# Zero-padded K and V, four one-bank score buffers and a fused feed-forward stage in a retention + SoLU kernel

## The chip, the cores and the metric

The kernel runs on one core of one Trainium2 chip. Times are device microseconds (us) of that core. PE is TensorE's matmuls, PEld its weight loads, DVE is VectorE, ACT is ScalarE, POOL is GpSimd. A run counts as faster or slower when it differs by more than 2% from the kernel before.

## The reference, cut to what matters

Retention (attention with a decay mask and no softmax) over 8 batches, 8 heads, 576 positions and a head size of 64, then a feed-forward part over the 4608 tokens: 512 → 1024, SoLU, LayerNorm, 1024 → 512.

```python
scores = (q @ k.T) / sqrt(64)                      # per batch and head, 576 x 576
ret    = scores * where(i >= j, gamma[h] ** (i - j), 0)
attn   = ret @ v                                   # 576 x 64
x      = attn of all heads side by side            # 4608 x 512
h      = x @ w_in                                  # 4608 x 1024
solu   = h * softmax(h)
ln     = (solu - mean) / sqrt(var + 1e-6) * g_ln
out    = ln @ w_out                                # 4608 x 512
```

## The kernel before

For each pair of heads the kernel transposes Q and K with PE into tiles whose partitions 0 to 63 hold one head and 64 to 127 the other. For each head it makes five key blocks of scores (the mask is causal, so block `kb` needs only `576 - 128*kb` columns), multiplies each by the decay table on DVE, and then makes the products with V ("PV" below) that add up in `opv`. The rows cut out are marked.

```python
tc.tile_pool(name="a_st", bufs=6) as a_st,
tc.tile_pool(name="ps_tr", bufs=2, space=bass.MemoryType.PSUM) as ps_tr,
tc.tile_pool(name="ps_sc", bufs=2, space=bass.MemoryType.PSUM) as ps_sc,   # two tiles of two banks
tc.tile_pool(name="ps_pv", bufs=1, space=bass.MemoryType.PSUM) as ps_pv,
# ... loads and casts of a batch, transposes and copies of a pair of heads cut ...
for hh in range(2):
    h = h0 + hh
    dr = slice(hh * D, (hh + 1) * D)              # 64 of the 128 partitions
    st_tiles = []
    for kb in range(SB):                          # SB = 5
        sps = ps_sc.tile([128, S], FP32, tag="sps")
        for c0 in range(0, ncols, 512):           # kb 0 needs 512 + 64 columns
            nc.tensor.matmul(out=sps[0:kb_rows, c0:c1],
                lhsT=kT[dr, 128 * kb:128 * kb + kb_rows],          # 64 rows x 128 columns
                rhs=qT[dr, 128 * kb + c0:128 * kb + c1], start=True, stop=True)
        st = a_st.tile([128, S], FP16, tag="st")
        nc.vector.tensor_tensor(out=st[0:kb_rows, 0:ncols], in0=sps[0:kb_rows, 0:ncols],
            in1=Mt[0:kb_rows, h, 0:ncols], op=ALU.mult)
        st_tiles.append(st)
    for kb in range(SB - 1):
        nc.tensor.matmul(out=opv[dr, 128 * kb:512],
            lhsT=v16[0:128, kb, h],                                # 128 rows x 64 columns
            rhs=st_tiles[kb][0:128, 0:512 - 128 * kb],
            start=(kb == 0), stop=(kb == SB - 2))
    # ... five matmuls of 64 columns into opv[dr, 512:S] cut ...
# ... after all batches: four groups of nine blocks of 128 tokens ...
#     stage 1 of each block: hps = x w_in (PE), exp (ACT), t = hps * e, statistics (DVE), transposes (PE)
#     then for the group: Ln and Exp (ACT), and for each block ops = lnT w_out (PE), osb (ACT), store
```

The softmax here doesn't subtract the row's maximum and nothing guards it: scores larger than these inputs give would overflow.

Of the kernel before, what the change touches and what calls it, by code (L numbers as in the profile page):

```python
# [17 lines left out]
def kernel(  # L18
# [10 lines left out]
    nc = tc.nc  # L29
# [47 lines left out]
    xT = const.tile([128, NDMB, NT], FP16)  # L77

    npart = 128
    with (  # L80
        tc.tile_pool(name="a_in", bufs=2) as a_in,
        tc.tile_pool(name="a_tr", bufs=4) as a_tr,
        tc.tile_pool(name="a_st", bufs=6) as a_st,
        tc.tile_pool(name="ps_tr", bufs=2, space=bass.MemoryType.PSUM) as ps_tr,
        tc.tile_pool(name="ps_sc", bufs=2, space=bass.MemoryType.PSUM) as ps_sc,
        tc.tile_pool(name="ps_pv", bufs=1, space=bass.MemoryType.PSUM) as ps_pv,
    ):
        for b in range(B):
            qn = a_in.tile([128, SB, H, D], FP32, tag="qn")
            kn = a_in.tile([128, SB, H, D], FP32, tag="kn")  # L90
            vn = a_in.tile([128, SB, H, D], FP32, tag="vn")
            q16 = a_in.tile([128, SB, H, D], FP16, tag="q16")
            k16 = a_in.tile([128, SB, H, D], FP16, tag="k16")
            v16 = a_in.tile([128, SB, H, D], FP16, tag="v16")
# [16 lines left out]
            nc.vector.tensor_copy(out=v16[:, 0:SB - 1], in_=vn[:, 0:SB - 1])  # L111
            nc.vector.tensor_copy(out=v16[0:SBL, SB - 1], in_=vn[0:SBL, SB - 1])

            for hp in range(HP):
                h0 = 2 * hp
                pass
                qT_ps = ps_tr.tile([128, S], FP16, tag="trps")
                kT_ps = ps_tr.tile([128, S], FP16, tag="trps")
# [9 lines left out]
                kT = a_tr.tile([128, S], FP16, tag="kT")  # L128
                nc.scalar.activation(out=qT, in_=qT_ps, func=ACT.Copy)
                nc.scalar.activation(out=kT, in_=kT_ps, func=ACT.Copy)  # L130

                opv = ps_pv.tile([128, S], FP32, tag="opv")
                for hh in range(2):
                    h = h0 + hh
                    dr = slice(hh * D, (hh + 1) * D)
                    pass
                    st_tiles = []
                    for kb in range(SB):
                        kb_rows = 128 if kb < SB - 1 else SBL
                        ncols = S - 128 * kb  # L140
                        sps = ps_sc.tile([128, S], FP32, tag="sps")
                        for c0 in range(0, ncols, 512):
                            c1 = min(ncols, c0 + 512)
                            nc.tensor.matmul(  # L144
                                out=sps[0:kb_rows, c0:c1],
                                lhsT=kT[dr, 128 * kb:128 * kb + kb_rows],
                                rhs=qT[dr, 128 * kb + c0:128 * kb + c1],
                                start=True, stop=True)
                        st = a_st.tile([128, S], FP16, tag="st")
                        nc.vector.tensor_tensor(  # L150
                            out=st[0:kb_rows, 0:ncols],
                            in0=sps[0:kb_rows, 0:ncols],
                            in1=Mt[0:kb_rows, h, 0:ncols],
                            op=ALU.mult)
                        st_tiles.append(st)
                    for kb in range(SB - 1):
                        nc.tensor.matmul(  # L157
                            out=opv[dr, 128 * kb:512],
                            lhsT=v16[0:128, kb, h],
                            rhs=st_tiles[kb][0:128, 0:512 - 128 * kb],  # L160
                            start=(kb == 0), stop=(kb == SB - 2))
                    for kb in range(SB):
                        kb_rows = 128 if kb < SB - 1 else SBL
                        nc.tensor.matmul(  # L164
                            out=opv[dr, 512:S],
                            lhsT=v16[0:kb_rows, kb, h],
                            rhs=st_tiles[kb][0:kb_rows, 512 - 128 * kb:S - 128 * kb],
                            start=(kb == 0), stop=(kb == SB - 1))
# [3 lines left out]
    GRP = 9  # L172
    ngrp = (NTB + GRP - 1) // GRP
    with (
        tc.tile_pool(name="m_sb", bufs=3) as m_sb,
        tc.tile_pool(name="m_ln", bufs=GRP + 2) as m_ln,
        tc.tile_pool(name="m_sc", bufs=4) as m_sc,
        tc.tile_pool(name="m_gs", bufs=2) as m_gs,
        tc.tile_pool(name="ps_h", bufs=4, space=bass.MemoryType.PSUM) as ps_h,
        tc.tile_pool(name="ps_ln", bufs=2, space=bass.MemoryType.PSUM) as ps_ln,  # L180
        tc.tile_pool(name="ps_o", bufs=2, space=bass.MemoryType.PSUM) as ps_o,
    ):
        for gi in range(ngrp):
            blocks = list(range(gi * GRP, min(NTB, (gi + 1) * GRP)))
            sqG = m_gs.tile([128, GRP], FP32, tag="sq")
            rstdG = m_gs.tile([128, GRP], FP32, tag="rstd")
            lnT_list = []
            for li, t in enumerate(blocks):
                tcols = slice(t * 128, (t + 1) * 128)
                e16 = m_sb.tile([128, DFF], FP16, tag="e16")  # L190
                t32 = m_sb.tile([128, DFF], FP32, tag="t32")
                zp = m_sc.tile([128, 2], FP32, tag="zp")
                stats = m_sc.tile([128, 2, 6], FP32, tag="stats")
                for c in range(2):
                    fcs = slice(c * 512, (c + 1) * 512)
                    hps = ps_h.tile([128, 512], FP32, tag="hps")
                    for i in range(NDMB):
                        nc.tensor.matmul(  # L198
                            out=hps, lhsT=xT[:, i, tcols],
                            rhs=w_in16[:, i, fcs],  # L200
                            start=(i == 0), stop=(i == NDMB - 1))
                    nc.scalar.activation(  # L202
                        out=e16[:, fcs], in_=hps, func=ACT.Exp,
                        accum_out=zp[:, c:c + 1])
                    nc.vector.tensor_tensor(  # L205
                        out=t32[:, fcs], in0=hps, in1=e16[:, fcs], op=ALU.mult)
                    nc.vector.bn_stats(out=stats[:, c], in_=t32[:, fcs])  # L207
                mv = m_sc.tile([128, 2], FP32, tag="mv")
                nc.vector.bn_aggr(out=mv, in_=stats)
                zs = m_sc.tile([128, 2], FP32, tag="zs")  # L210
                nc.vector.tensor_scalar(
                    out=zs[:, 0:1], in0=zp[:, 0:1], scalar1=zp[:, 1:2],
                    scalar2=1e-9, op0=ALU.add, op1=ALU.add)
                nc.scalar.activation(out=zs[:, 1:2], in_=zs[:, 0:1],
                                     func=ACT.Square)
                nc.vector.tensor_scalar(
                    out=sqG[:, li:li + 1], in0=zs[:, 1:2], scalar1=1e-6,
                    scalar2=mv[:, 1:2], op0=ALU.mult, op1=ALU.add)
                negmu = m_sc.tile([128, 1], FP32, tag="negmu")
                nc.vector.tensor_scalar(  # L220
                    out=negmu, in0=mv[:, 0:1], scalar1=-1.0, scalar2=None,
                    op0=ALU.mult)
                ln16 = m_sb.tile([128, DFF], FP16, tag="ln16")
                for c in range(2):
                    fcs = slice(c * 512, (c + 1) * 512)
                    nc.vector.tensor_scalar(  # L226
                        out=ln16[:, fcs], in0=t32[:, fcs], scalar1=negmu,
                        scalar2=None, op0=ALU.add)
                lnT_ps = ps_ln.tile([128, NFFB, 128], FP16, tag="lnT")
                for f in range(NFFB):  # L230
                    nc.tensor.transpose(  # L231
                        out=lnT_ps[:, f], in_=ln16[:, f * 128:(f + 1) * 128],
                        identity=ident)
                lnT = m_ln.tile([128, NFFB, 128], FP16, tag="lnTs")
                nc.scalar.activation(out=lnT, in_=lnT_ps, func=ACT.Copy)  # L235
                lnT_list.append(lnT)
            nblk = len(blocks)
            lnv = m_gs.tile([128, GRP], FP32, tag="lnv")
            nc.scalar.activation(out=lnv[:, 0:nblk], in_=sqG[:, 0:nblk],
                                 func=ACT.Ln)  # L240
            nc.scalar.activation(out=rstdG[:, 0:nblk], in_=lnv[:, 0:nblk],
                                 func=ACT.Exp, scale=-0.5)
            for li, t in enumerate(blocks):
                tcols = slice(t * 128, (t + 1) * 128)
                lnT = lnT_list[li]
                ops = ps_o.tile([128, DM], FP32, tag="ops")
                for f in range(NFFB):
                    nc.tensor.matmul(  # L248
# [36 lines left out]
```

## Time and profile before

| | us |
|---|---|
| timed, median of 3 runs | 542.65 (540.79 to 542.81) |
| profiled span | 536.3 |
| loading, to the first decay product | 43 |
| attention (43 to 349) | 306 |
| feed-forward (349 to 536) | 187 |

The page of the kernel before: the span, the busy time of each engine, the clock granted to TensorE in 40 slices (tenths of full speed), and the costliest groups. A group's columns are line, engine, operation, output and input, shapes, count; then busy us and mean ns of one; then the idle time before them and what ended it.

```profile
span 536.3 us, 6044 instructions
PE 437.5 (82%) x2144; PEld 195.2 (36%) x2144; DVE 295.3 (55%) x704; ACT 226.9 (42%) x401; POOL 0.2 (0%) x4
PEclk9999999999999999999999999999989999999959
L150 DVE TENSOR_TENSOR st<-sps,Mt 128x576 f16<-128x576 f32 (+4 forms) x320 | 149.7, 487 | 160.5 <-PE sps L144 151.5
L144 PE MATMUL sps<-qT,kT 64*128 64x512 f16 (+5 forms) x384 | 136.8, 406 | 20.3 <-DVE st L150 20.3
L157 PE MATMUL opv<-st,v 128*64 128x512 f16 (+3 forms) x256 | 106.2, 474 | 5.5 <-DVE v L111 5.5
```

The windows view of the kernel before, attention in the first line and feed-forward in the second. Its columns are the stretch and its length; busy us and count of PE, PEld, DVE, ACT and POOL; the granted clock; the busy share of the DMA engines; GB/s.

```profile
43.00:349.00 306.00, 280.26 (x1266) 120.58 (x1265) 161.41 (x336) 91.92 (x121) 0.00 (x0) 1.00 0.45 82
349.00:536.30 187.30, 154.53 (x865) 73.03 (x864) 129.95 (x360) 122.84 (x269) 0.00 (x0) 0.95 0.14 51
```

The timeline of the kernel before, PE alone. Its columns are start us, length us, engine, line, operation, output and input, tile (rows x columns of the array), input shape and count.

```profile
49.19 1.27 PE L157 MATMUL opv<-st,v 128*64 128x512 f16 x4 [0.47 <-DVE v L111]
...
329.60 0.63 PE L157 MATMUL opv<-st,v 128*64 128x512 f16 x1
330.17 0.34 PE L144 MATMUL sps<-qT,kT 64*128 64x192 f16 x1
330.44 0.53 PE L157 MATMUL opv<-st,v 128*64 128x384 f16 x1
330.89 0.26 PE L144 MATMUL sps<-qT,kT 64*64 64x64 f16 x1
...
376.41 1.89 PE L198 MATMUL hps<-w_in,xT 128*128 128x512 f16 x8 [0.29 <-DVE t L205]
```

PE is 280.26 of 306 us "busy" in attention, yet the starts are far apart: a PV of 512 columns starts at 329.60 and the score matmul after it at 330.17, 0.57 us later. In the feed-forward part eight matmuls of 512 columns take 1.89 us, the last of them 0.38, so they start (1.89 − 0.38)/7 = 0.216 us apart. The page and the windows show the clock in attention as full (9, 1.00). The first line of the timeline shows four PV matmuls (512, 384, 256 and 128 columns) taking 1.27 us.

### The profile page before, as it was taken

The page shows a single profiled execution, that of the slowest core. Times are in us where ns is not written, and L with a number is a line of the kernel's source. Part 1 is how long each engine was busy: PE and PEld are TensorE (multiplying, and loading weights), DVE is VectorE, ACT ScalarE, POOL GpSimd, SP SyncE. Part 2 cuts the span into 40 slices and gives each one's busy share as a digit, 9 for nine tenths or more (in the row PEclk, how much of TensorE's full clock was granted, in tenths as well). Part 3 has the DMA queues.
Part 4 walks back from the last instruction along what each step waited for, and adds up shares of the span by engine and source line. Part 5 has one row for each costly group of instructions (what it writes and reads, how often), then busy time and mean ns, then how long its engine had stood idle before and what let it go on. Part 6 is the DMA issues. An engine that isn't in the chain of part 4 may idle for free.

```text
span 536.3 us, 6044 instructions
## 1 busy us (share of the span) xinstructions
PE 437.5 (82%) x2144; PEld 195.2 (36%) x2144; DVE 295.3 (55%) x704; ACT 226.9 (42%) x401; POOL 0.2 (0%) x4
## 2 busy tenths in 40 slices
PE   0009998998998998998989988898699789879756
PEld 0004333343443343343344343344244334434322
DVE  0204555536545546545555545579937984984920
ACT  2134333243143152341332330066847777676653
POOL 0000000000000000000000000000000000000000
PEclk9999999999999999999999999999989999999959
DMA  9599999454444444444000000000030021022013
GB/s 301 190 204 215 209 216 198 86 111 88 88 90 88 89 88 89 88 89 89 0 2 0 1 1 0 1 0 2 8 144 26 2 109 68 1 90 90 0 55 122
DMA packets 121678, 44.74 MB, mean 83 GB/s; under 512 B 114480, under 2 KB 114480, under 8 KB 121648
## 3 DMA queue, kind: packets, MB, share of 16 engines
q1 hardware_dynamic: 121648, 44.35, 37.6%
q8 instruction: 17, 0.28, 0.2%
q14 instruction: 13, 0.11, 0.1%
HBM read 34.90 MB, written 9.44 MB: 83 GB/s over the span
## 4 chain that ended last, share of the span: by engine, by line
PE 63%; DVE 17%; ACT 6%; DMA 5%; issue 5%; SPq 4%; DVEq 0%; ACTq 0%
PE opv L157 17%; PE sps L144 17%; PE ops L248 11%; DVE st L150 5%; PE opv L164 5%; PE hps L198 4%; PE qT_ps L121 4%; PE kT_ps L124 4%; DMA wt<-in_moe_w_out_dram 3%; DVE stats L207 3%; SPq L98 3%; DVE t L205 3%; DVE ln L226 3%; ACT lnT L235 2%; DVE v L111 2%
## 5 line engine op out<-in xcount | busy, mean ns | idle before, releaser
L150 DVE TENSOR_TENSOR st<-sps,Mt 128x576 f16<-128x576 f32 (+4 forms) x320 | 149.7, 487 | 160.5 <-PE sps L144 151.5
L144 PE MATMUL sps<-qT,kT 64*128 64x512 f16 (+5 forms) x384 | 136.8, 406 | 20.3 <-DVE st L150 20.3
L157 PE MATMUL opv<-st,v 128*64 128x512 f16 (+3 forms) x256 | 106.2, 474 | 5.5 <-DVE v L111 5.5
L169 ACT ACTIVATE xT<-opv 128x576 f16<-128x576 f32 x32 | 20.8, 650 | 160.3 <-PE opv L164 160.3
L248 PE MATMUL ops<-w_out,lnT 128*128 128x512 f16 x288 | 71.3, 395 | 11.0 <-ACT osb L252 9.9
L198 PE MATMUL hps<-w_in,xT 128*128 128x512 f16 x288 | 71.7, 382 | 9.5 <-DVE t L205 6.1
L205 DVE TENSOR_TENSOR t<-hps,e 128x512 f32<-128x512 f32 x72 | 47.2, 660 | 27.0 <-ACT e L202 27.0
L157 PEld LDWEIGHTS <-v 128*64 128x64 f16 x256 | 29.0, 135 | 79.0 <-issue 58.1
L121 PE MATMUL qT_ps<-ident,q 128*128 128x128 f16 (+1 forms) x160 | 27.3, 292 | 35.7 <-ACT q L103 35.7
L144 PEld LDWEIGHTS <-kT 64*128 64x128 f16 (+1 forms) x384 | 35.6, 115 | 56.1 <-issue 49.6
L202 ACT ACTIVATE e<-hps 128x512 f16<-128x512 f32 x72 | 42.9, 600 | 22.8 <-PE hps L198 21.2
L207 DVE BATCH_NORM_STATS2 stats<-t 128x6 f32<-128x512 f32 x72 | 48.3, 685 | 0.0
L248 PEld LDWEIGHTS <-lnT 128*128 128x128 f16 x288 | 28.8, 101 | 42.9 <-issue 13.1
L198 PEld LDWEIGHTS <-xT 128*128 128x128 f16 x288 | 27.6, 98 | 41.2 <-issue 15.1
L164 PE MATMUL opv<-st,v 128*64 128x64 f16 (+1 forms) x320 | 41.2, 249 | 0.0
L164 PEld LDWEIGHTS <-v 128*64 128x64 f16 (+1 forms) x320 | 32.7, 158 | 17.7 <-issue 13.5
L235 ACT ACTIVATE lnT<-lnT_ps 128x1024 f16<-128x1024 f16 x36 | 36.2, 1022 | 5.3 <-PE lnT_ps L231 4.7
L130 ACT ACTIVATE kT<-kT_ps 128x576 f16<-128x576 f16 x32 | 20.8, 650 | 36.7 <-PE kT_ps L124 36.7
L252 ACT ACTIVATE osb<-ops,rstdG 128x512 f32<-128x512 f32 x36 | 24.5, 688 | 27.1 <-PE ops L248 24.1
L231 PE MATMUL lnT_ps<-ident,ln 128*128 128x128 f16 x288 | 26.5, 225 | 7.4 <-DVE ln L226 6.7
L121 PEld LDWEIGHTS <-q 128*128 128x128 f16 (+1 forms) x160 | 14.4, 123 | 49.8 <-ACT q L103 35.7
L226 DVE TENSOR_SCALAR ln<-t,negmu 128x512 f16<-128x512 f32 x72 | 31.3, 477 | 0.2
(28 smaller groups left out, 204.6 us busy)
## 6 DMA issues: line engine op xcount, KB each, us to landing
out_dram<-osb SPq DMA_DIRECT2D x36, 256.0 KB, 2.0
qn<-in_q_dram SPq DMA_DIRECT2D x32, 256.0 KB, 4.9
kn<-in_k_dram SPq DMA_DIRECT2D x32, 256.0 KB, 5.0
vn<-in_v_dram SPq DMA_DIRECT2D x32, 256.0 KB, 4.8
Mt<-decay_tab SPq DMA_DIRECT2D x1, 2304.0 KB, 8.7
wt<-in_moe_w_in_dram SPq DMA_DIRECT2D x4, 512.0 KB, 6.6
wt<-in_moe_w_out_dram SPq DMA_DIRECT2D x8, 256.0 KB, 3.7
qn<-in_q_dram SPq DMA_DIRECT2D x8, 128.0 KB, 4.7
```

The source lines that it names most:

```text
L121: nc.tensor.transpose(out=qT_ps[:, 128 * c:128 * c + rows], in_=q16[0:rows, c, h0:h0 + 2], identity=ident[0:rows, 0:rows])
L144: nc.tensor.matmul(out=sps[0:kb_rows, c0:c1], lhsT=kT[dr, 128 * kb:128 * kb + kb_rows], rhs=qT[dr, 128 * kb + c0:128 * kb + c1], start=Tru ...
L150: nc.vector.tensor_tensor(out=st[0:kb_rows, 0:ncols], in0=sps[0:kb_rows, 0:ncols], in1=Mt[0:kb_rows, h, 0:ncols], op=ALU.mult)
L157: nc.tensor.matmul(out=opv[dr, 128 * kb:512], lhsT=v16[0:128, kb, h], rhs=st_tiles[kb][0:128, 0:512 - 128 * kb], start=(kb == 0), stop=(kb ...
L164: nc.tensor.matmul(out=opv[dr, 512:S], lhsT=v16[0:kb_rows, kb, h], rhs=st_tiles[kb][0:kb_rows, 512 - 128 * kb:S - 128 * kb], start=(kb == ...
L198: nc.tensor.matmul(out=hps, lhsT=xT[:, i, tcols], rhs=w_in16[:, i, fcs], start=(i == 0), stop=(i == NDMB - 1))
L202: nc.scalar.activation(out=e16[:, fcs], in_=hps, func=ACT.Exp, accum_out=zp[:, c:c + 1])
L205: nc.vector.tensor_tensor(out=t32[:, fcs], in0=hps, in1=e16[:, fcs], op=ALU.mult)
L207: nc.vector.bn_stats(out=stats[:, c], in_=t32[:, fcs])
L226: nc.vector.tensor_scalar(out=ln16[:, fcs], in0=t32[:, fcs], scalar1=negmu, scalar2=None, op0=ALU.add)
L235: nc.scalar.activation(out=lnT, in_=lnT_ps, func=ACT.Copy)
L248: nc.tensor.matmul(out=ops, lhsT=lnT[:, f], rhs=w_out16[:, f], start=(f == 0), stop=(f == NFFB - 1))
```

## The change

The intent is that every matmul use the full 128x128 array (the last key block of a head has only 64 keys and keeps narrow tiles), that PE run ahead of DVE, and that feed-forward work sit between batches. Four parts:

1. **Padding.** K of each head is copied into a tile of 128 rows whose other 64 rows are zero; V gets 128 columns of which 64 are zero. Scores then use all of Q's 128 rows (the other head's rows meet zeros), and both heads of a pair add up into one `opv` of 128 partitions.
2. **Score buffers.** Two score tiles of two banks become four of one bank; the 576-column block is cut into 512 + 64 with a decay product each. `hps` and `ops` share these four.
3. **Fusion.** One scope of pools; a feed-forward group of nine blocks follows every second batch.
4. Smaller: fp32 inputs in one buffer instead of two, `m_sb` 3 → 2, a pool of four for `osb`.

```diff
+    v16z = [const.tile([128, SB, HP, 2, 2 * D], FP16, name=f"v16z{n}") for n in range(2)]   # memset to 0
+    kz = [[const.tile([128, S], FP16, name=f"kz{hh}{n}") for n in range(NZ)] for hh in range(2)]  # memset to 0
-        tc.tile_pool(name="ps_sc", bufs=2, space=bass.MemoryType.PSUM) as ps_sc,
+        tc.tile_pool(name="ps_big", bufs=4, space=bass.MemoryType.PSUM) as ps_big,
+        def moe_group(blocks):  # ... the feed-forward part, moved here; hps and ops from ps_big, cut ...
...
-                nc.scalar.activation(out=kT, in_=kT_ps, func=ACT.Copy)
+                for hh in range(2):
+                    r = slice(hh * D, (hh + 1) * D)
+                    nc.scalar.activation(out=kzs[hh][r], in_=kT_ps[r, 0:S], func=ACT.Copy)
...
-                        sps = ps_sc.tile([128, S], FP32, tag="sps")
                         for c0 in range(0, ncols, 512):
+                            sps = ps_big.tile([128, 512], FP32, tag="big")
-                                lhsT=kT[dr, 128 * kb:128 * kb + kb_rows],
-                                rhs=qT[dr, 128 * kb + c0:128 * kb + c1],
+                                lhsT=kzs[hh][:, 128 * kb:128 * kb + kb_rows],
+                                rhs=qT[:, 128 * kb + c0:128 * kb + c1],
-                        nc.vector.tensor_tensor(out=st[0:kb_rows, 0:ncols], ...)     # once for each kb
+                            nc.vector.tensor_tensor(out=st[0:kb_rows, c0:c1], ...)   # once for each c0
...
-                            out=opv[dr, 128 * kb:512],
-                            lhsT=v16[0:128, kb, h],
-                            start=(kb == 0), stop=(kb == SB - 2))
+                            out=opv[:, 128 * kb:512],
+                            lhsT=v16[0:128, kb, hp, hh],
+                            start=(kb == 0 and hh == 0), stop=(kb == SB - 2 and hh == 1))
...
+            if b % 2 == 1:
+                blk0 = (b - 1) * S // 128
+                moe_group(list(range(blk0, blk0 + GRP)))
```

## The prediction

> **What bounds the kernel now.** The span is 536 us (timed 542.65). By the timeline: 43 us of loading, 306 us of attention (43 to 349; 38.6 us a batch: 8 heads of about 4.25 us plus 4 for casts and transposes), 187 us of feed-forward (groups of nine blocks, 42 to 53 us each). In attention PE shows as 93% busy, but is not streaming. A head's eight large matmuls have 2,752 columns; at the feed-forward part's 0.216 us per 512 columns that is 1.16 us, plus seven small ones and five transposes at 0.1: 2.3 us, against 4.25. The timeline shows why: wherever a score matmul (64x128 tile) meets a PV matmul (128x64 tile), the next start is late. PV 512 to score: 0.56 us; PV 384: 0.46; score 192 to PV: 0.27, though 192 columns need 0.08. Five PV matmuls of one shape start 0.1 us apart. The Trainium skill ("TensorEngine Tiling (Array Packing)", Key Properties) says that changing the tiling mode drains TensorE; this trace agrees, at 0.2 to 0.35 us a change. By the waits view DVE is idle 151 us for scores, PE 20 us for the only two score buffers.
>
> **What the change does.** (1) K and V are zero-padded, so every matmul is a 128x128 tile: same columns, no mode changes. (2) Four one-bank score tiles instead of two; the 576-column product becomes 512 + 64, about 0.15 us more DVE per head. (3) Two half-height K copies for one: +0.65 us ACT per pair, not critical. (4) A feed-forward group follows every second batch. By the instruction order, DVE and PE still do attention, then group, then attention; this hides little and loses something: today group n+1's first blocks run during group n's output matmuls. (5) Single-buffered f32 inputs: casts stay a batch ahead, no cost.
>
> **Estimate.** From the trace: score to DVE start 0.29 us after streaming, DVE end to PE 0.05, DVE 0.69/0.22/0.62/0.49/0.36/0.22 (2.3 back to back). Order: score 512, 64, 448, PV 512, score 320, PV 384, score 192, PV 256, score 64, PV 128, five small PVs. Following it: DVE starts at 0.50, PV 512 at 1.24, PV 384 at 1.97, PV 256 at 2.41, PV 128 at 2.91, next head at 3.47. So 3.5 us a head, bound by the PE-DVE-PE loop, transposes fitting in its waits. A batch: 28 + 2 for casts = 30; attention 240 (-66).
>
> Feed-forward: DVE-bound at 3.63 us a block, 33 us; table loads 3, about 39 remaining output matmuls 8.5, next transposes, copies and first score 3.5, entry 2: 50 each, 202 in all (+15).
>
> Sum: 43 + 240 + 202 = 485 span, plus 5 as today: **488 us**, range **455 to 517**. Chances: faster by over 2% 0.95, within 2% 0.04, slower 0.01.
>
> **What would show it.** Right: score-to-PV spacing falls to columns/2.4 GHz where nothing is waited for; a head takes 3.3 to 3.7 us; DVE idle on scores falls to about 70 us; PE's waits on the decay product become the limit; DVE has gaps of 12 to 16 us at each group-to-attention switch; DVE busy about 310 us. Wrong: spacing unchanged (drains not the cause); head time near 2.6 (loop hidden, total near 440); group over 55 us.
>
> **What would make it wrong.** Transposes landing on the loop (+0.5 us a head, +30 us); strided V casts slower; lower granted clock after the waits; ACT blocked behind casts waiting for DMA; better overlap at group borders than read from the order.

## The result, and the profile after

| | before | after |
|---|---|---|
| timed, median | 542.63 us (537.3 to 544.17, 15 runs) | 409.25 us (405.62 to 411.94, 12 runs) |
| profiled span | 536.3 | 403.6 |
| attention | 306 | 167.2, in four stages |
| feed-forward | 187.3 | 193.4, in four stages |

The ratio is 0.7562 (0.7532 to 0.7592). Every ratio here is the mean time of one kernel's fast runs over that of the other's of the same rounds, so it isn't quite the ratio of the medians quoted. The prediction said 488 us, with a range from 455; the change gained much more than that.

The page of the kernel after, the same lines as above.

```profile
span 403.6 us, 6141 instructions
PE 311.4 (77%) x2144; PEld 164.4 (41%) x2144; DVE 284.5 (70%) x784; ACT 243.6 (60%) x433; POOL 13.0 (3%) x14
L241 DVE TENSOR_TENSOR st<-sps,Mt 128x512 f16<-128x512 f32 (+5 forms) x384 | 138.6, 425 | 74.7 <-PE sps L236 70.0
L236 PE MATMUL sps<-qT,kz 128*128 128x512 f16 (+5 forms) x384 | 89.6, 287 | 4.4 <-DVE st L241 2.8
L248 PE MATMUL opv<-st,v16z 128*128 128x512 f16 (+3 forms) x256 | 69.6, 300 | 6.3 <-ACT xT L260 4.9
```

The same counts of score and PV matmuls take a third less busy time each (136.8 → 89.6 and 106.2 → 69.6). DVE's idle time for scores fell from 151.5 to 70.0 us, PE's waits for a decay product from 20.3 to 2.8. The 70.0 us are mostly not in attention's loop: 16.8 are the wait for the very first scores (16.7 in before) and 39.5 the three changes from a group back to attention. What is left, 13.8 us, was 134.8 in before.

The windows view of the kernel after: attention of two batches and a feed-forward group in turn (the first two of the four rounds).

```profile
43.00:88.20 45.20, 40.34 (x302) 23.21 (x303) 37.59 (x104) 27.70 (x37) 0.00 (x0) 1.00 1.12 190
88.20:136.80 48.60, 39.44 (x238) 18.96 (x237) 34.02 (x94) 36.50 (x75) 0.00 (x0) 1.00 0.58 130
136.80:178.20 41.40, 38.57 (x313) 22.21 (x310) 37.64 (x104) 27.73 (x39) 0.00 (x0) 1.00 0.81 141
178.20:226.70 48.50, 39.83 (x229) 18.76 (x227) 33.94 (x96) 31.63 (x70) 0.00 (x0) 0.96 0.45 103
```

All four attention stages take 45.2 + 41.4 + 40.2 + 40.4 = 167.2 us, the four groups 48.6 + 48.5 + 46.7 + 49.6 = 193.4. In attention PE and DVE are now both close to full: 38.57 and 37.64 of 41.40 us.

The timeline of the kernel after: PE over one head.

```profile
62.31 0.38 PE L248 MATMUL opv<-st,v16z 128*128 128x512 f16 x1 [0.22 <-ACT xT L260]
62.62 0.22 PE L236 MATMUL sps<-qT,kz 128*64 128x64 f16 x1
62.77 0.34 PE L248 MATMUL opv<-st,v16z 128*128 128x384 f16 x1
62.94 0.38 PE L236 MATMUL sps<-qT,kz 128*128 128x512 f16 x1
63.16 0.27 PE L248 MATMUL opv<-st,v16z 128*128 128x256 f16 x1
63.27 0.19 PE L236 MATMUL sps<-qT,kz 128*128 128x64 f16 x1
63.29 0.22 PE L248 MATMUL opv<-st,v16z 128*128 128x128 f16 x1
63.35 0.41 PE L255 MATMUL opv<-st,v16z 128*128 128x64 f16 x5
63.70 0.36 PE L236 MATMUL sps<-qT,kz 128*128 128x448 f16 x1
```

The score matmuls of 512 and 64 columns at 62.94 and 63.27 are the *next* head's: they stand between this head's PV matmuls. Its 448-column scores follow at 63.70, before any of its own PVs. So DVE has the next head's scores in hand before this head is done. (The tile of 128x64 at 62.62 is the block of 64 keys: the padding doesn't widen it.) The timeline of the kernel after, DVE alone, shows it:

```profile
136.84 2.13 DVE L241 TENSOR_TENSOR st<-sps,Mt 128x512 f16<-128x512 f32 x6 [12.76 <-PE sps L236]
...
159.26 17.34 DVE L241 TENSOR_TENSOR st<-sps,Mt 128x512 f16<-128x512 f32 x48
```

Forty-eight decay products, eight heads of six, run in 17.34 us without an idle stretch: 2.17 us a head. The prediction had 3.5. (The first line shows the gap of 12.76 us at a change from a group back to attention, which the prediction did expect.)

### The clock records

The trace also holds the throttle's own records. Each says from when, for how long, and at which share of full speed. The first ones of four kernels, in us from the start of the span (worked out from the trace's nanoseconds; this is no profile view):

```
before   350.7 for 37.5 at 1.0;  388.3 for 3.4 at 0.5;  391.7 for 116.1 at 1.0; ...
after     48.4 for 167.3 at 1.0; 215.7 for 3.4 at 0.5;  219.1 for 184.3 at 1.0
e1        46.6 for 238.9 at 1.0; ...      (padding alone; below)
e2       328.7 for 34.1 at 1.0; ...       (buffers alone; its attention ends near 324)
```

Before's first record comes 1.8 us after the first 128x128 feed-forward matmul, at the *end* of attention. After's comes 5 us after attention starts. Nothing is recorded before the first one, and the page shows such a time as full speed. The starts say what the clock was. Medians of the distance from start to start, without waits:

```
same shape, 512 columns: PV to PV in attention of before         0.427 us   = 1.2 columns a ns
                         feed-forward matmuls of before and after 0.216 us   = 2.4 columns a ns
                         PV and feed-forward, in stretches recorded at 0.5   0.427 us
```

The Trainium skill, "TensorE: Matmul & The Clock Gate", Part 1 (The HAM clock gate), gives 426.7 ns cold and 215.7 ns warm for back-to-back matmuls of 512 columns, and says that "the default state is throttled, and activity releases the throttle". The two spacings here agree with its two figures. So a theory suggested itself that the prediction doesn't have: **all of attention before ran at half clock**. The line `49.19 1.27 ... x4` above says so without any record; e9 below tests it.

### The profile page after: what moved, and what is told of

It reads as the page before. It is cut to its first block, busy times and chain, and to the rows that moved or that the text cites. A ratio compares the mean times of both kernels' runs of the same rounds, so it can differ in the third digit from the quotient of the medians.

```text
span 403.6 us, 6141 instructions
## 1 busy us (share of the span) xinstructions
PE 311.4 (77%) x2144; PEld 164.4 (41%) x2144; DVE 284.5 (70%) x784; ACT 243.6 (60%) x433; POOL 13.0 (3%) x14
## 4 chain that ended last, share of the span: by engine, by line
PE 35%; DVE 27%; ACT 18%; issue 8%; DMA 7%; SPq 4%; ACTq 0%; DVEq 0%
PE ops L168 14%; PE opv L248 7%; DVE stats L122 7%; DVE t L120 7%; PE sps L236 6%; DVE st L241 5%; ACT kz L222 5%; DVE ln L141 5%; DMA wt<-in_moe_w_out_dram 4%; ACT xT L260 4%; ACT qT L218 2%; PE opv L255 2%; SPq L186 2%; PE kT_ps L214 2%; PE qT_ps L211 2%
## 5 line engine op out<-in xcount | busy, mean ns | idle before, releaser
L241 DVE TENSOR_TENSOR st<-sps,Mt 128x512 f16<-128x512 f32 (+5 forms) x384 | 138.6, 425 | 74.7 <-PE sps L236 70.0
L236 PE MATMUL sps<-qT,kz 128*128 128x512 f16 (+5 forms) x384 | 89.6, 287 | 4.4 <-DVE st L241 2.8
L168 PE MATMUL ops<-w_out,lnT 128*128 128x512 f16 x288 | 67.4, 386 | 13.1 <-ACT osb L172 8.4
L248 PE MATMUL opv<-st,v16z 128*128 128x512 f16 (+3 forms) x256 | 69.6, 300 | 6.3 <-ACT xT L260 4.9
L260 ACT ACTIVATE xT<-opv 128x576 f16<-128x576 f32 x32 | 20.7, 648 | 52.6 <-PE opv L255 52.6
L117 ACT ACTIVATE e<-hps 128x512 f16<-128x512 f32 x72 | 42.7, 595 | 13.8 <-PE hps L113 13.2
L211 PE MATMUL qT_ps<-ident,q 128*128 128x128 f16 (+1 forms) x160 | 21.4, 226 | 37.8 <-ACT q L191 36.0
L236 PEld LDWEIGHTS <-kz 128*128 128x128 f16 (+1 forms) x384 | 32.5, 100 | 39.0 <-issue 22.8
L222 ACT ACTIVATE kz<-kT_ps 64x576 f16<-64x576 f16 x64 | 41.1, 642 | 9.4 <-PE kT_ps L214 8.5
L248 PEld LDWEIGHTS <-v16z 128*128 128x128 f16 x256 | 24.1, 97 | 16.5 <-issue 5.7
L146 PEld LDWEIGHTS <-ln 128*128 128x128 f16 x288 | 18.5, 97 | 20.2 <-DVE ln L141 16.6
L255 PE MATMUL opv<-st,v16z 128*128 128x64 f16 (+1 forms) x320 | 26.5, 194 | 0.0
```

Of the source, the lines that this page charges most:

```text
L117: nc.scalar.activation(out=e16[:, fcs], in_=hps, func=ACT.Exp, accum_out=zp[:, c:c + 1])
L146: nc.tensor.transpose(out=lnT_ps[:, f * 128:(f + 1) * 128], in_=ln16[:, f * 128:(f + 1) * 128], identity=ident)
L168: nc.tensor.matmul(out=ops, lhsT=lnT[:, f], rhs=w_out16[:, f], start=(f == 0), stop=(f == NFFB - 1))
L211: nc.tensor.transpose(out=qT_ps[:, 128 * c:128 * c + rows], in_=q16[0:rows, c, h0:h0 + 2], identity=ident[0:rows, 0:rows])
L222: nc.scalar.activation(out=kzs[hh][r], in_=kT_ps[r, 0:S], func=ACT.Copy)
L236: nc.tensor.matmul(out=sps[0:kb_rows, 0:c1 - c0], lhsT=kzs[hh][:, 128 * kb:128 * kb + kb_rows], rhs=qT[:, 128 * kb + c0:128 * kb + c1], st ...
```

## The experiments

Four explanations of the gain were tested: the clock, which the wide tiles raise; the changes of shape themselves, of which the padding takes away about half; the four score buffers, which let PE run a head ahead; and the fusion. All twelve kernels gave correct results. Before was run again in each set of rounds, with medians between 541.56 and 542.09 us. Medians and ranges take in all runs; the runs marked slow (one of after, two of e4, one of e12) are left out of the ratios.

| kernel | median us | range | ratio to before (95%) |
|---|---|---|---|
| after | 409.25 | 405.62 to 411.94 | 0.7562 (0.7532 to 0.7592) |
| e1 padding alone | 441.31 | 437.51 to 443.08 | 0.8174 (0.8122 to 0.8227) |
| e2 four buffers alone | 516.38 | 512.89 to 519.01 | 0.9548 (0.9489 to 0.9607) |
| e3 padding and four buffers | 415.10 | 413.86 to 415.79 | 0.7676 (0.7640 to 0.7712) |
| e4 the same with two one-bank buffers | 474.55 | 468.04 to 483.65 | 0.8710 (0.8626 to 0.8795) |
| e5 after, K padded, V narrow | 424.74 | 424.38 to 425.09 | 0.7851 (0.7802 to 0.7901) |
| e6 after, V padded, K narrow | 461.33 | 460.59 to 461.58 | 0.8525 (0.8461 to 0.8590) |
| e7 after, half groups | 426.27 | 424.47 to 427.20 | 0.7875 (0.7822 to 0.7929) |
| e8 after, outputs spread over attention | 432.52 | 431.42 to 433.39 | 0.7994 (0.7942 to 0.8046) |
| e9 before, burst ahead of attention | 541.79 | 537.05 to 542.43 | 0.9984 (0.9936 to 1.0032) |
| e10 before, burst and a wide matmul per head | 571.32 | 570.74 to 572.99 | 1.0553 (1.0512 to 1.0595) |
| e11 after, burst ahead of attention | 411.67 | 408.80 to 412.86 | 0.7592 (0.7560 to 0.7624) |
| e12 after, DVE relieved | 397.47 | 393.98 to 400.15 | 0.7314 (0.7275 to 0.7352) |

### e1: the padding alone

```diff
 # before, plus
+v16z, kz: tiles memset to 0, filled as in the change; lhsT=kzs[hh][...], rhs=qT[:, ...], out=opv[:, ...]
 # ps_sc stays at two tiles of two banks; no fusion
```

> The kernel before with zero-padded K and V only; two two-bank score tiles and the separate feed-forward scope stay. By its instruction order each head is again issued score 512, 64, 448, 320, PV 512, score 192, PV 384, score 64, PV 256 and so on, the very order that the prediction assumed. Theory A (drains cost PE time, but with two score buffers a head stays bound by the PE-DVE-PE loop): about 3.4 to 3.5 us a head, attention about 240 us, time about 475 us. Rival B (padding alone makes attention DVE-bound): 2.2 to 2.5 us a head, attention about 175 us, time about 410 us. Rival C (drains do not matter): about 540 us.

Measured: 441.31 us, three quarters of the whole gain (101 of 133 us). Attention takes 203.5 us instead of 306, feed-forward 189.2. The first clock record is at 46.6 us, 4 us into attention.

The expectation calls the order it starts from "the very order" of the prediction. That was not so, as the trace shows. The timeline of e1, PE, one head:

```profile
162.12 0.61 PE L157 MATMUL sps<-qT,kz 128*128 128x512 f16 x3
...
163.39 0.30 PE L157 MATMUL sps<-qT,kz 128*128 128x320 f16 x1 [0.66 <-DVE st L163]
163.53 0.38 PE L170 MATMUL opv<-st,v16z 128*128 128x512 f16 x1
163.92 0.24 PE L157 MATMUL sps<-qT,kz 128*128 128x192 f16 x1
...
165.01 0.61 PE L157 MATMUL sps<-qT,kz 128*128 128x512 f16 x3
```

A head in the steady part takes 165.01 − 162.12 = 2.89 us here; following the loop, the prediction had 3.47. The scores of 320 columns start *ahead* of PV 512 and those of 192 ahead of PV 384, each one PV earlier than the prediction assumed. The trace of before has the same order as e1 (in the lines above, 192 columns follow PV 512 at 330.17), so it was there to be read. The loop PE–DVE–PE is real with two buffers (the 0.66 us wait), but shorter than it was sized.

### e2: the four one-bank buffers alone

```diff
-tc.tile_pool(name="ps_sc", bufs=2, space=bass.MemoryType.PSUM) as ps_sc,
+tc.tile_pool(name="ps_sc", bufs=4, space=bass.MemoryType.PSUM) as ps_sc,
 for c0 in range(0, ncols, 512):
+    sps = ps_sc.tile([128, 512], FP32, tag="sps")       # and a decay product for each c0
```

> The kernel before with four one-bank score tiles and the 512 + 64 split only, no padding. Its instruction order puts the next head's scores between this head's PV matmuls, as in the changed kernel, with about 8 changes of tile shape a head. Theory A (drains bound PE once the look-ahead is there): about 4 us a head, time 515 to 545 us. Rival (the look-ahead alone brings the gain): about 415 us.

Measured: 516.38 us, ratio 0.9548. Attention takes about 281 us (−25), a steady head 3.82 us instead of 4.25. In the profiled run the first clock record comes after attention has ended. The other three runs list mean clocks of 0.983, 0.818 and 0.745, and two of them, 516.53 us at 0.818 and 516.22 at 0.745, took the same time: the mean says how much was recorded, not how fast PE ran. Running ahead helps, but at half clock PE itself is the limit: it is busy for 277 of the 281 us.

### e3: both

```diff
 # the edits of e1 and e2 together; feed-forward still after all batches
```

> The kernel before with padding and four one-bank score tiles; all attention still runs ahead of all feed-forward, double-buffered f32 inputs. Theory A (padding and look-ahead together are the whole gain): attention about 170 us, feed-forward 187 us as before, time 400 to 410 us, no slower than the changed kernel. Rival (putting the groups between batches hides work): about 430 us or more.

Measured: 415.10 us. Attention takes 179.5 us, feed-forward 189.5. From e1 to e3 the buffers save 24 us of attention, as many as from before to e2 (25). All the rest of the change, the fusion with it, is worth 0.7676 → 0.7562, 1.5%, less than the 2% that count as a difference here: attention 179.5 → 167.2 and feed-forward 189.5 → 193.4. The stretches of attention in which e3's DMA engines are hardly busy (178 to 222 us, DMA share 0.01) take 44 us for two batches, as the ones with much DMA do (45). So it isn't DMA traffic that the fusion relieves. That it hides casts and transposes at the borders between batches behind the groups fits the numbers, but no run separates it.

### e4: both, with only two one-bank buffers

```diff
-tc.tile_pool(name="ps_sc", bufs=4, space=bass.MemoryType.PSUM) as ps_sc,
+tc.tile_pool(name="ps_sc", bufs=2, space=bass.MemoryType.PSUM) as ps_sc,   # otherwise e3
```

> The previous kernel with two instead of four one-bank score tiles. Theory A (the number of score buffers sets the order and so the loop): 3.3 to 3.5 us a head, time about 470 us. Rival (the smaller one-bank tiles and the 512 + 64 split matter, not their number): about 405 us.

Measured: 474.55 us, slower than e1, whose two buffers hold two banks each. Here the 512 + 64 columns of one block take up both tiles, and PE can't start another block until DVE has freed one. The clock is lost as well, most likely through PE's waits (it is busy for 193 of 245 us of attention; no run separates this): the profiled run, marked as slow, has a mean clock of 0.913, and its first record of full clock comes 20 us after attention starts. In the stretches at full clock a steady head takes 3.32 us, in those recorded at 0.5 it takes 4.21. By the ratios, which leave the slow runs out, the count of the buffers is worth about 56 us (0.8710 against 0.7676), but part of that is clock. So the run shows that the gain of e3 lies in the number of the buffers, not in their size, and can't say how much for itself.

### e5: after, with V narrow again

```diff
 # after, but
-lhsT=v16[0:128, kb, hp, hh], out=opv[:, 128 * kb:512]
+lhsT=v16[0:128, kb, h],      out=opv[dr, 128 * kb:512]
```

> The changed kernel with K padded but V not: scores are 128x128 tiles, PV stays 128x64, so the shape still changes at every step from scores to PV and back; the instruction order is nearly that of the changed kernel. Theory A (it is the change of shape that costs): nearly all of the loss comes back, 3.6 to 3.9 us a head, time 490 to 515 us. Rival D (each narrow tile is slow by itself, and half the padding gives half the gain): about 455 us, and the mate run about the same. Rival E (only the 64-row K tiles are slow): about 410 us.

Measured: 424.74 us. Scores and PV still differ in shape (128x128 against 128x64). Counted in the traces, score and PV matmuls that follow each other differ in shape 397 times here, 426 times in before and 225 times in after, where the blocks of 64 keys still do. The clock is full from 52.6 us on, but for 3.4 us. The timeline of e5, PE:

```profile
174.93 0.39 PE L230 MATMUL sps<-qT,kz 128*128 128x512 f16 x1
175.25 0.30 PE L242 MATMUL opv<-st,v 128*64 128x256 f16 x1
```

The distance is 0.32 us where the same shape has 0.216: a change of shape costs 0.10 us. Keeping nearly all changes of shape costs e5 15.5 us against after, of which the narrow V's own effects can't be told apart (an estimate: 172 more changes at 0.10 us are 17 us). The other 118 of the 133 us of gain are there with the changes of shape kept.

### e6: after, with K narrow again

```diff
 # after, but
-lhsT=kzs[hh][:, 128 * kb:...], rhs=qT[:, ...]
+lhsT=kT[dr, 128 * kb:...],     rhs=qT[dr, ...]
```

> The changed kernel with V padded but K not: scores are 64x128 tiles, PV 128x128. Theory A: again 490 to 515 us. Rival D: about 455 us. Rival F (only the 128x64 PV tiles are slow, as their weight loads are longest): about 410 us.

Measured: 461.33 us. This kernel is a comparison in itself, since it runs part of its attention at either clock. Its records: none until 110.3 us (its first two batches are over before that), then full to 161.5 but for 3.4 us, half for 64.9 us, then full from 226.4 on, again but for 3.4 us. The timeline of e6, PE, in the stretch recorded at half clock, and then in one at full:

```profile
193.76 0.60 PE L229 MATMUL sps<-qT,kT 64*128 64x512 f16 x1
194.29 0.40 PE L241 MATMUL opv<-st,v16z 128*128 128x256 f16 x1
...
197.35 0.60 PE L229 MATMUL sps<-qT,kT 64*128 64x512 f16 x1
...
302.34 0.39 PE L229 MATMUL sps<-qT,kT 64*128 64x512 f16 x1
302.66 0.28 PE L241 MATMUL opv<-st,v16z 128*128 128x256 f16 x1
...
304.62 0.39 PE L229 MATMUL sps<-qT,kT 64*128 64x512 f16 x1
```

One instruction sequence, one kernel: a head takes 197.35 − 193.76 = 3.59 us at half clock and 304.62 − 302.34 = 2.28 at full. Means over pairs of steady heads are 3.57 and 2.44. From the first decay product to the last, its four attention stages take 64.0, 62.2, 41.8 and 43.1 us: the first two at half clock, the others at full. Once up, the clock stayed up through a stage here; once down, it didn't come back within one. The windows view of e6 shows the recorded clock of both stretches (the third value from the end):

```profile
180.00:190.00 10.00, 10.00 (x52) 4.21 (x50) 4.84 (x12) 2.86 (x6) 0.00 (x0) 0.50 0.39 81
300.00:310.00 10.00, 9.27 (x62) 4.19 (x61) 9.06 (x27) 3.61 (x4) 0.00 (x0) 1.00 0.00 1
```

At half clock PE is busy all of the time and DVE half of it; at full clock both are busy for nine tenths. A change of shape costs the same at either clock: 0.537 us instead of 0.427 from a 512-column score to a PV at half, 0.319 instead of 0.216 at full.

### e7: after, with groups of five and four blocks

```diff
-                moe_group(list(range(blk0, blk0 + GRP)))
+                cut = (0, 5, 9)
+                for lo, hi in zip(cut[:-1], cut[1:]):
+                    moe_group(list(range(blk0 + lo, blk0 + hi)))
```

> The changed kernel with each group of nine blocks cut in five and four, so that the output matmuls of the first five can run while VectorE works on the other four. Theory: only four blocks' output matmuls (7 us of 15.5) are left exposed at each of the four group ends; the DVE gap of 12.5 to 14 us falls to 8 to 10 us, time 385 to 397 us. Rival: the four extra pairs of activation table loads and PE contention eat it up: 405 us or more.

Measured: 426.27 us, slower. The hope was that the second half's stage 1 would fill the end of the first. But the first half's output matmuls stand ahead of the second half's hidden ones, and in the trace PE runs them in that order (the first group's last outputs until 117.5 us, hidden ones from there). The waits view of e7 and of after, DVE for `e` (total us, times, longest):

```profile
DVE t L120 <- ACT e L117: 38.1, 9, 9.5
```

```profile
DVE t L120 <- ACT e L117: 4.6, 4, 2.0
```

There are twice as many ends of groups, and at seven of them DVE is now idle for 6.8 to 9.5 us, against three times 12.5 to 14.2 in after.

### e8: after, with a group's output matmuls spread over the next two batches

```diff
+                if pend is not None:            # at the start of each pair of heads
+                    moe_out(pend, OUTMAP[j])    # 0, 1, 1, 2, 1, 1, 1 and 2 blocks
...
-                moe_group(list(range(blk0, blk0 + GRP)))
+                pend = moe_group(list(range(blk0, blk0 + GRP)))
```

> The changed kernel with a group's output matmuls moved into the next two batches, one block ahead of each head pair. In attention PE (about 2.15 us a head by its starts) and DVE (2.17 us) are about equally loaded, so the 15.5 us of output matmuls have to be paid there; only the waits around them go. Theory: the three DVE gaps of 12.5 to 14 us shrink to about 5, attention grows by about 3 to 4 us a group, time 385 to 398 us. Rival (PE has room in attention): about 375 us. Rival (PE has none, and score buffers are held by outputs): 405 us or more.

Measured: 432.52 us, slower. DVE's waits for scores rose from 70.0 to 95.8 us, since PE is as loaded as DVE in attention and has no room for more. And without the output matmuls PE idles at the end of each group, which costs the clock: after each of the three groups that attention follows, 13.7 us are recorded at half clock (from 120.1, 215.7 and 311.3 us). Between 120 and 125 us PE is busy for 1.31 of 5 us.

### e9: before, with a burst of wide matmuls ahead of attention

```diff
+warm = ps_sc.tile([128, S], FP32, tag="sps")
+for _ in range(48):
+    nc.tensor.matmul(out=warm[:, 0:512], lhsT=ident, rhs=w_out16[:, NFFB - 1], start=True, stop=True)
 for b in range(B):
```

> The kernel before, with 48 full-array matmuls of no use (128x128 on 512 columns) while the loads run, just ahead of attention; nothing else changes. The earlier traces suggest that the kernel before runs all of attention with TensorE at half clock, since consecutive 512-column PV matmuls of one shape start 0.427 us apart there and 0.215 apart elsewhere. Theory G (the clock, not the shape change, is the main cost, and it holds once raised): starts of 0.215 us, about 3.4 us a head in place of 4.25, attention about 240 us, time 465 to 485 us. Theory H (the clock is the cost, but narrow tiles cannot hold it): it falls back to half within a few tens of us of the start of attention, time 525 to 542 us. Rival I (the shape change drains, the clock is not the matter): 540 us with starts unchanged from the first head on.

Measured: 541.79 us, the same as before. The purpose was a record of the clock in before's attention. The page's row of the clock of e9, then its windows view (burst, attention, first feed-forward group):

```profile
PEclk9996555555555555555555555589989999999959
```

```profile
30.00:43.60 13.60, 10.66 (x62) 5.08 (x59) 0.32 (x1) 6.58 (x7) 0.00 (x0) 1.00 1.34 214
43.60:349.00 305.40, 279.51 (x1262) 120.24 (x1260) 161.13 (x336) 91.75 (x120) 0.00 (x0) 0.50 0.45 82
351.00:388.00 37.00, 28.75 (x176) 13.87 (x175) 36.02 (x98) 27.76 (x67) 0.00 (x0) 1.00 0.00 1
```

The burst raised the clock for 13.7 us. Its own matmuls, all of one shape, start 0.427 us apart before the first record (at 29.9 us) and 0.216 after it: time without records is half clock here. After the burst PE waits 2.5 us for casts; the clock fell as attention began, and stayed at half for all of it although PE was busy for 279.51 of 305.40 us, 92%. The spacing (0.427 us), the busy time and the total are those of before, where nothing was recorded. So before's attention ran at half clock: shown. A warm start doesn't help: these narrow tiles don't win the clock back. Whether they would have held it without the wait, the run doesn't say.

### e10: e9, with one wide matmul of 512 columns per head

```diff
+                            if c0 == 0 and kb == 0:
+                                nc.tensor.matmul(out=sps[:, 0:512], lhsT=ident, rhs=w_out16[:, 0], start=True, stop=True)
```

> The previous kernel with one more useless full-array matmul of 512 columns before each head's first score, into the same tile, which the real score then overwrites. It adds 0.22 us (full clock) or 0.43 us (half clock) of PE and one shape change a head. Theory G or H with enough full-array work to hold the clock: about 3.6 to 3.8 us a head, time 480 to 500 us, faster than before with more work. If even that does not hold the clock: about 4.7 us a head, time 560 us or more.

Measured: 571.32 us. A head has 3,200 columns of scores and PV, so 512 of 3,712, 14%, were now on the full array. The clock still fell at 43.4 us and stayed at half for 337.9 us. The 64 extra matmuls cost 29.5 us, 0.46 each: half clock again.

### e11: after, with the burst

```diff
+warm = ps_big.tile([128, 512], FP32, tag="big")
+for _ in range(48): ...      # as in e9
```

> The changed kernel with the same 48 useless matmuls ahead of attention. Its clock record begins only 5 us into attention. Theory G: the first batch starts at full clock, 1 to 3 us saved, time 406 to 408 us where the changed kernel has 409. Rival: no difference, or a loss if the burst ends late.

Measured: 411.67 us, no gain over after. Here too PE waits 2.5 us for casts and the clock fell once attention began (at 44.8 us), so the fall isn't due to narrow tiles. But it came back after 13.7 us and stayed for the rest of that stage. That is the other half of e9: with wide tiles the attention recovers the clock by itself, with narrow ones it doesn't.

### e12: after, with work taken off DVE

```diff
-                nc.vector.tensor_copy(out=v16[...], in_=vnv[...])
+                nc.gpsimd.tensor_copy(out=v16[...], in_=vnv[...])
...
+                else:                       # the second half of ln16
+                    nc.scalar.activation(out=ln16[:, fcs], in_=t32[:, fcs], func=ACT.Identity, bias=negmu)
```

> The changed kernel with VectorE relieved: the casts of V go to GpSimd (1.75 us of DVE a batch) and one of the two halves of the subtraction of the mean goes to ScalarE (about 0.39 us of DVE a block of 3.63). Theory: after the change DVE is the bound both in attention and in the feed-forward blocks, so about 6 us of casts and about 10 us of subtraction come off, time 390 to 400 us. Rival (other waits or the clock set the pace, or ScalarE and GpSimd become late): 405 us or more.

Measured: 397.47 us, the fastest of all, 3.3% under after by the two ratios (0.7314/0.7562 = 0.967). DVE is busy for 259.4 us instead of 284.5, ACT for 263.0 instead of 243.6, POOL for 35.0 instead of 13.0. That DVE sets the pace is confirmed for the feed-forward blocks: from its first product `t` to its last, a group takes 26.2 to 27.2 us instead of 28.8 to 30.7. The four attention stages together, from first to last decay product, take 159.5 us instead of 161.6 without the casts of V; there PE is as loaded, and this run doesn't show DVE as the limit.

## Why the prediction was wrong, point by point

The time was outside the range: 409.25 us, against 488 (455 to 517). By stages, the prediction's 240 us of attention became 167.2, its 202 of feed-forward 193.4, its 43 of loading 43. So 73 of the 81 us too much are in attention, in the one term "3.5 us a head".

- **The step that failed: "Following it: ... next head at 3.47. So 3.5 us a head, bound by the PE-DVE-PE loop".** Two errors, both in "Order: score 512, 64, 448, PV 512, score 320, PV 384, ...". By the author's account it was taken from a list of instructions without their shapes; the matmuls were put in the wrong places.
  - With two buffers, each later score matmul stands one PV earlier. The loop takes 2.89 us (e1), 0.58 less. (Not all of that need be the order: e1 keeps the 576 columns in one product.)
  - With four buffers the order is another: the next head's 512 and 64 columns run between this head's PVs. The loop across a head is hidden, and a steady head takes 2.16 us on the mean of pairs, 0.73 less again. The DVE timeline line with 48 products in 17.34 us is the direct reading. 64 heads x (3.47 − 2.16) = 84 us, an estimate from the steady heads; the stages show 73, since a batch takes 20.9 us, 3.6 more than eight steady heads, where the prediction added 2.
- **"+0.15 us more DVE per head", "2.3 back to back", "DVE busy about 310 us": wrong.** DVE needs 2.17 us a head, split product included, and was busy for 284.5 us. Records of back-to-back products overlap (six at a mean of 425 ns are 2.55 us, but take 2.17), and adding lone durations counts the overlap twice.
- **"PE's waits on the decay product become the limit": wrong.** They fell to 2.8 us. DVE and PE are about equally loaded.
- **"this trace agrees, at 0.2 to 0.35 us a change": wrong in size and in cause.** The Trainium skill ("TensorEngine Tiling (Array Packing)", Key Properties) says "Mode switching requires drain", and that holds: 0.10 to 0.14 us a change. But the prediction subtracted spacings at 2.4 columns a ns from starts at 1.2 columns a ns, so most of its "drain" was half clock. A check was at hand: PV matmuls of one shape in the same stage, where no drain is possible, were 0.427 us apart. Since the estimate of the kernel after used the full rate anyway, this error gave a wrong reason, not the wrong number. ("Five PV matmuls of one shape start 0.1 us apart" hid it: four of the five start 0.054 us apart, 1.2 columns a ns again, and the fifth has another shape.)
- **"score-to-PV spacing falls to columns/2.4 GHz": right, but no test.** Both explanations foresaw it. The test named as "Wrong: spacing unchanged (drains not the cause)" would not have told them apart either.
- **"DVE idle on scores falls to about 70 us": right by luck.** It is 70.0, but the prediction had a loop that leaves DVE idle in every head (3.5 us against 2.3), and listed the gaps after groups apart. Those gaps and the first wait make 56.2 of the 70.0; the loop leaves 13.8.
- **Right:** "gaps of 12 to 16 us at each group-to-attention switch" (12.76, 14.21 and 12.53); "no cost" of single-buffered inputs is at least not contradicted; feed-forward about 50 us a group (46.7 to 49.6). The last term of "What would show it", "head time near 2.6 (loop hidden, total near 440)", named the right alternative, and the kernel went past it.

Where the 139 us of attention came from, by the stages of four profiled runs:

| step | attention us | saved |
|---|---|---|
| before | 306 | |
| padding (e1): full clock, and fewer changes of shape (235 for 426) | 203.5 | 102.5 |
| four buffers (e3): PE a head ahead | 179.5 | 24 |
| the rest of the change (after) | 167.2 | 12.3 |

Of the padding's part, the clock is by far the larger: e5 keeps the changes of shape and loses only 15.5 us in all. An estimate: 191 fewer changes at 0.10 to 0.14 us are 19 to 27 us, which leaves about 80 to the clock; in e6 half clock costs about 20 us in each of two stages, and attention has four. What exactly the clock's monitor weighs stays open. K wide and V narrow (e5) opened the clock at 52.6 us, K narrow and V wide (e6) only some of the time, both narrow (before, e2, e10) never in attention. In e5 and e6 half of the columns are on the full array, so the share of wide columns alone doesn't decide it. The padded rows and columns are zeros, so the clock opened without useful values in them.

## What to carry to other kernels

Before explaining late starts of matmuls by any mechanism, take the spacing of two matmuls of *one* shape in the *same* stage, and work out columns per ns: a half rate there was the clock here, whatever a row of the page showed for a time without records. Here a matmul that used half of the array cost twice, once in unused rows or columns and once in a clock that never opened, so zero padding that adds no columns to stream can pay for itself. And when an order of instructions decides an estimate, read it with its shapes, and ask for each buffer added which later instruction it lets run ahead.

## What the Trainium skill lacked or had wrong

- "TensorE: Matmul & The Clock Gate", Part 1 and "Why this matters for your kernels": it advises to keep TensorE busy for 4 us or more to get the full clock. That isn't enough: with tiles of 64x128 and 128x64 PE was 92% busy for 305 us and got half clock throughout (e9; before has the same spacing). The page doesn't say that a stage of such narrow tiles can stay at half clock, however busy.
- The same page: a warm-up burst doesn't help such a stage. 48 wide matmuls raised the clock for 13.7 us; it fell as attention began, with narrow tiles and with wide ones, and narrow ones didn't win it back (e9, 541.79 against 542.63 us; no gain in e11 either).
- The same page, caveats on the trace's records: it calls the events unreliable. What misled here was their absence: nothing is recorded ahead of the first change, and the profile shows that time as full speed, 306 us of it in before.
- "TensorEngine Tiling (Array Packing)", Key Properties: it says that changing the mode drains TensorE, and gives no figure. Here it is 0.10 to 0.11 us a change at either clock (0.319 against 0.216 us, and 0.537 against 0.427), up to 0.14 from a PV to a score in before (0.565 against 0.427).
